# Order of the constants at the start of attention, and the place of the next expert's count

## The chip, the cores and the metric

The kernel runs on one core of a Trainium2 chip. The metric is the device time of one execution in microseconds (us); the median over several runs is compared. A profile of one further execution shows what each engine did: TensorE (PE; its weight loads are shown apart as PEld), VectorE (DVE), ScalarE (ACT), GpSimd (POOL) and the queue of SyncE (SP), which issues most transfers. A name with a q behind it (PEldq, ACTq) is the engine's sequencer, which fetches instructions, branches and loads registers.

## What is computed

Attention with a window and a few sink tokens, and behind it a mixture of experts with one expert for each token:

```python
# q, k, v: (4, 8, 768, 64); n_sink 4, window 128
scores = q @ k.T / 8
keep = (key < n_sink) | ((query - key >= 0) & (query - key < window))
a = softmax(where(keep, scores, -1e9))
x = (a @ v) as (3072, 512)              # token by token, heads side by side

logits = x @ w_gate                     # (3072, 8)
e = argmax(logits); gate = softmax(logits)[e]
y = gate * (relu(x @ w1[e]) @ w2[e])    # w1: 512 x 1024, w2: 1024 x 512
```

All of it is float32. A product in the experts is made of three: each operand is split into a high part (rounded) and the rest, and high x high, high x rest and rest x high are added.

## The kernel before

**Attention.** The 3072 tokens are 24 groups of 128 queries (`g`), and each group has 8 heads in two quads. For a head TensorE computes the scores into one of four PSUM banks `s` (`qk`, L189); VectorE scales them, applies a mask and takes the row's extreme in one custom instruction into `smask` (`softmax`, L203); ScalarE takes the exponential (`exp`, L210); TensorE transposes the result (`tp`, L231) and multiplies by the values (`pv`, L274). The scores of the next quad need the banks that the softmax step of this quad has read. Behind it come norms, the gate's logits and, for batches of groups, the routing: which expert each token goes to and at which place.

The softmax step needs a mask tile: `m0` for the first block of a sequence, `m1` for the second, `m2` for all others. They are built by VectorE (`Constants.mask`, L467) from `win` and `sk` (`window`, L461), which need the numbers `n_sink` and `window` as floats (`numbers`, L447), which a small DMA brings (`num`, L509), the first of SP's queue. VectorE also makes constants that only later steps use: `routing` (L491: `tri`, `iota8`, `four`, `tok`, `slots`) for the routing, and `vbd` (L499), which the sink values need. GpSimd makes the index patterns (`iotas`, `more_iotas`), fills some tiles (`fills`, L487) and sets `rows0` to zero (L1172), the tile into which the experts' rows are later gathered.

**The planner.** The order of all this is not written by hand. Each step is put into a `Plan` with a rank, the steps it waits for, and a cost for each engine that may do it (`t` TensorE, `v` VectorE, `a` ScalarE, `p` GpSimd, `s` SP). `Plan.order` walks in time over a model with these costs: at each point it takes the engine that can start first, and of the steps ready for it the one with the lowest rank. The instructions are then issued in that order, and each engine runs its own in that order. Steps that become ready at another point of the model may change the order on every engine behind them. The experts' constants have rank 14.5, the masks -7.5, 0.5 and 8.5, the softmax step -3 and more with each head, and the zeroing 18.5.

**The experts.** Behind attention and an early part of expert 0 (256 of its tokens), `run` goes through the 8 experts. The number of tokens of an expert, in units of 32, is known only on the chip. It stands in the tile `m`, and each of the five engines has a register for it. `tc.Switch(R[e], ...)` (L1063) branches to the body that was made for this number (0 to 32 units), on each engine by itself. `load_units(e)` (L813) gives one register load to each of the five engines (L816; the profile calls it TENSOR_LOAD). `regs` loads the count of expert 0 ahead of all bodies, and the body of expert `e` loads the count of expert `e + 1` as its first instruction; the last body loads none.

A body with up to 4 units is `narrow`; up to 16 units it is one `chunk`; with more it is two chunks, the first with `first=True`. A chunk first calls `begin` (evacuation of the previous expert's sums by ScalarE and VectorE, L1005 and L1007, and their scatter by GpSimd, four indirect DMAs, L1037). Then it goes over 8 slices of the hidden dimension: `l1` is 12 products of one slice (L889), a relu on ScalarE (L893) and its rest on VectorE (L895); `l2`, four slices behind, is the second product (L905). Between them `own` and `ahead` split the weights of this or the next expert (ScalarE L666, VectorE L674) and start the next load into the raw tile (SP, L661), and `turn_rows` transposes the rows of the next expert (L872) and, on GpSimd, gathers those of the one after. `narrow` does the same with tokens and hidden dimension exchanged (`first(p)`, L963).

## Time and profile before

| | |
|---|---|
| median of 3 runs | 559.08 us (558.99 to 561.92) |
| the profiled execution | 559.36 us, span 557.6 us |
| granted TensorE clock, mean | 0.969 |
| attention and routing | up to about 208 us |
| early part of expert 0 | to about 223.8 us |
| bodies of experts 0 to 7, first product at | 226.75, 255.60, 323.41, 360.36, 407.36, 443.64, 470.78, 528.86 us |
| last TensorE work to the end of the span | about 16 us |

In the rows shown below a time is in us from the start of the span. A row of the order in time has start, duration, engine, line, operation, output <- inputs and, in brackets, how long the engine was idle before and what the profile holds to have ended that. A row by line (L816) has the count, the shortest, middle and longest duration in ns, and the first and last start. A row of a stretch (A:B) has its length, each engine's busy time with the number of instructions, then the granted clock of TensorE (1.00 is full), the busy share of the DMA engines and GB/s.

### The profile page before, as it was taken

Reading aid. Unit: us, or ns where it says so; the run is one execution under the profiler, and the core shown is the slowest. Engines: PE = TensorE matmul, PEld = TensorE weight load, DVE = VectorE, ACT = ScalarE, POOL = GpSimd, SP = SyncE. Lnnn points to the kernel's source line nnn. Section 1 sums busy time; section 2 is a strip of 40 time slices with the busy share of each in tenths; the row PEclk is TensorE's granted clock in tenths of the full one; section 3 lists DMA queues with packets and bytes.
Section 4 is the critical chain, followed back from the end, with each engine's and each line's share of the span. In section 5 each row is a group of like instructions: output and inputs, shape, how many; then the busy total and the mean of one; then the engine's idle time right before and its main releaser. Section 6 shows DMA issues by size and latency. Waiting matters only on the chain.

```text
span 557.6 us, 12015 instructions
## 1 busy us (share of the span) xinstructions
PE 513.3 (92%) x4182; PEld 423.8 (76%) x4182; DVE 325.0 (58%) x1105; ACT 289.3 (52%) x813; POOL 127.5 (23%) x171
## 2 busy tenths in 40 slices
PE   5999999999999899798999989899989898999980
PEld 3667777777777688787989789788788696998670
DVE  8797788888797955463316356264156283526230
ACT  2889888988988812353215254263155172425240
POOL 3222330120104414425012032121032133210020
PEclk9899999999999999799999999999989999999996
DMA  8778764543432106474106436254247375310010
GB/s 261 239 253 250 224 192 143 148 146 117 142 113 59 39 21 204 140 229 118 58 19 205 136 132 203 87 183 127 66 136 256 93 237 151 103 42 2 8 46 21
DMA packets 48494, 74.57 MB, mean 134 GB/s; under 512 B 7130, under 2 KB 19418, under 8 KB 48288
## 3 DMA queue, kind: packets, MB, share of 16 engines
q1 hardware_dynamic: 42208, 59.05, 33.7%
q0 software_dynamic: 6080, 13.39, 8.1%
q14 instruction: 151, 1.24, 0.9%
q8 instruction: 55, 0.90, 0.8%
HBM read 63.23 MB, written 15.73 MB: 142 GB/s over the span
## 4 chain that ended last, share of the span: by engine, by line
PE 69%; issue 10%; DVE 7%; DMA 7%; ACT 5%; POOL 1%; another core or an unknown queue 0%; DVEq 0%; ACTq 0%; POOLq 0%
PE hp L889 23%; PE y L905 20%; DMA out<-ys,oi 7%; PE s L189 6%; PE pt L231 6%; PE xps L274 6%; PE tp L872 2%; ACT pn L210 2%; PE xps L290 2%; PE m L286 1%; ACT ptc L140 1%; DVE wl L674 1%; PE m L410 1%; DVE smask L203 1%; PE xps L261 1%
## 5 line engine op out<-in xcount | busy, mean ns | idle before, releaser
L889 PE MATMUL hp<-xh,wh 128*128 128x288 f32 (+6 forms) x288 | 93.9, 326 | 14.2 <-DVE ys L1005 7.5
L210 ACT ACTIVATE pn<-smask,sm 128x260 f32<-128x260 f32 (+1 forms) x192 | 92.7, 485 | 16.5 <-DVE sm L203 16.1
L674 DVE TENSOR_TENSOR wl<-wraw,wh 128x512 fp32r<-128x512 f32 x117 | 81.0, 706 | 26.1 <-ACT wh L666 23.3
L889 PE MATMUL hp<-xh,wl 128*128 128x288 f32 (+6 forms) x288 | 92.7, 322 | 0.0
L889 PE MATMUL hp<-xl,wh 128*128 128x288 f32 (+6 forms) x288 | 92.6, 322 | 0.0
L905 PE MATMUL y<-wh,hh 128*128 128x512 f32 (+2 forms) x224 | 91.1, 407 | 0.0
L893 ACT ACTIVATE hh<-hp 128x256 fp32r<-128x256 f32 (+6 forms) x80 | 34.2, 428 | 108.1 <-PE hp L889 100.7
L905 PE MATMUL y<-wh,hl 128*128 128x512 f32 (+2 forms) x224 | 88.1, 393 | 0.0
L905 PE MATMUL y<-wl,hh 128*128 128x512 f32 (+2 forms) x224 | 87.9, 392 | 0.0
L895 DVE SCALAR_TENSOR_TENSOR hl<-hp,hh 128x256 fp32r<-128x256 f32 (+6 forms) x80 | 38.1, 477 | 79.8 <-ACT hh L893 70.4
L666 ACT ACTIVATE wh<-wraw 128x512 fp32r<-128x512 f32 x116 | 70.5, 625 | 25.0 <-PE y L905 24.2
L889 PEld LDWEIGHTS hp<-xh,wh 128*128 128x128 f32 x288 | 58.2, 202 | 20.1 <-issue 17.2
L203 DVE CUSTOM_DVE_ANT_0 smask<-s,m 128x260 f32<-128x260 f32 (+1 forms) x192 | 69.3, 398 | 6.6 <-PE s L189 4.8
L1037 POOL DMA_INDIRECT out<-ys,oi x34 | 34.9, 1025 | 155.4 <-ACT ys L1007 147.0
L889 PEld LDWEIGHTS hp<-xl,wh 128*128 128x128 f32 x288 | 58.0, 201 | 2.1
L889 PEld LDWEIGHTS hp<-xh,wl 128*128 128x128 f32 x288 | 57.9, 201 | 0.9
L189 PE MATMUL s<-keys,q 64*64 64x196 f32 (+2 forms) x768 | 52.1, 346 | 5.5 <-DVE sm L203 5.1
L858 POOL DMA_INDIRECT rows<-rows,tl x32 | 32.6, 1018 | 86.5 <-PE tp L872 70.8
L231 PE MATMUL pt<-ident,pn 128*128 128x128 f32 x352 | 49.1, 280 | 0.8 <-ACT pn L210 0.3
L905 PEld LDWEIGHTS y<-wh,hl 128*128 128x128 f32 (+2 forms) x224 | 39.5, 176 | 12.2
L905 PEld LDWEIGHTS y<-wl,hh 128*128 128x128 f32 (+2 forms) x224 | 39.7, 177 | 10.1
L905 PEld LDWEIGHTS y<-wh,hh 128*128 128x128 f32 (+2 forms) x224 | 39.6, 177 | 9.2
(207 smaller groups left out, 758.2 us busy)
## 6 DMA issues: line engine op xcount, KB each, us to landing
wraw<-in_w SPq DMA_DIRECT2D x128, 256.0 KB
keys<-in_k SPq DMA_DIRECT2D x24, 264.0 KB
q<-in_qp SPq DMA_DIRECT2D x24, 256.0 KB
v<-in_v SPq DMA_DIRECT2D x24, 256.0 KB
rows<-row SPq DMA_DIRECT2D x24, 256.0 KB
out<-ys,oi POOLq DMA_INDIRECT x34
rows<-rows,tl POOLq DMA_INDIRECT x32
vs<-in_vs SPq DMA_DIRECT2D x4, 24.0 KB
```

What stands on the lines that cost most here:

```text
L189: nc.tensor.matmul(self.s[h % 4][o, a:z], self.q[g][rows, hp, o], self.keys[rows, hp, at + a:at + z], start=True, stop=True)
L203: nc.vector.tensor_tensor_reduce(t[:, :w], s[:, :w], m, -0.125, 3.0e38, OP.add, OP.min, sm[:, 0, h:h + 1])
L210: self.nc.scalar.activation(self.pn[g][:, h, :w], t[:, :w], AF.Exp, bias=sm[:, 0, h:h + 1], scale=-1.0, accum_out=sm[:, 1, h:h + 1])
L231: nc.tensor.transpose(t[:, h % 2, j, :], self.pn[g][:, h, c:c + 128], self.cons["ident"])
L274: nc.tensor.matmul(self.xps[r * 64:(r + 1) * 64, hp, :], self.v[g + d][:, h * 64:(h + 1) * 64], t[:, r, j, :], start=(j == 0 and hp == 0), ...
L666: self.nc.scalar.activation(w, r, AF.Copy)
L674: {"v": self.nc.vector, "p": self.nc.gpsimd}[e].tensor_tensor(w, r, self.wh[k][:, u % FT].bitcast(F32), op=OP.subtract)
L889: nc.tensor.matmul(p[:, :n], w[:, dd], x[b][:, d, :n], start=(i == 0), stop=(i == 11))
L893: nc.scalar.activation(hh[:, :n], p[:, :n], AF.Relu)
L895: nc.vector.scalar_tensor_tensor(hl[:, :n], p[:, :n], 0.0, hh[:, :n].bitcast(F32), op0=OP.max, op1=OP.subtract)
L905: nc.tensor.matmul(y, h[:, j * 128:j * 128 + w], x, start=(f == 0 and k == 0), stop=(f == FT - 1 and k == 2))
L1037: st = nc.gpsimd.indirect_dma_start(out=self.out, out_offset=bass.IndirectOffsetOnAxis(ap=ids[:, j:j + 1], axis=0), in_=self.ys[k][:, j, : ...
```

## The change

Three steps of the plan get one more step to wait for. The experts' constants `routing` and `vbd` wait for the third mask, `("m", 2)`; the zeroing of `rows0` waits for the first exponential of group 1, `("exp", 1, 0)`. Costs and ranks stay as they are. And `load_units(e + 1)` goes from the head of `expert` into `chunk`, behind `l1` of slice 0 of the first chunk, and into `narrow`, behind `first(0)`.

```diff
-        put(("c", "route"), self.routing, "c", 14, [("c", "rel"), ("c", "more"), ("c", "fill")], args=(), v=500)
-        put(("c", "vbd"), self.vbd, "c", 14, [("c", "more")], args=(), v=1600)
+        put(("c", "route"), self.routing, "c", 14, [("c", "rel"), ("c", "more"), ("c", "fill"), ("m", 2)], args=(), v=500)
+        put(("c", "vbd"), self.vbd, "c", 14, [("c", "more"), ("m", 2)], args=(), v=1600)
...
         for f in range(FT):
             if n:
                 self.l1(e, f, b, n)
+            if first and f == 0:
+                self.load_units(e + 1)
             if first and 1 <= f <= BEHIND:
                 self.own(e, FT - BEHIND - 1 + f)
...
         self.begin(e)
         first(0)
+        self.load_units(e + 1)
         for f in range(FT - BEHIND, FT):
             self.own(e, f)
...
     def expert(self, e, m):
         last = e + 1 == E
-        self.load_units(e + 1)
         nxt = None if last else (0, (e + 1) % 2, 4)
...
-    put(("zero",), lambda: moe.nc.gpsimd.memset(moe.rows[0], 0.0), "w1", 0, args=(), p=2500)
+    put(("zero",), lambda: moe.nc.gpsimd.memset(moe.rows[0], 0.0), "w1", 0, [("exp", 1, 0)], args=(), p=2500)
```

## The prediction

> **What bounds the kernel now.** I read the page first, then the table of stretches, then the instructions in order of time, last the sequencer's own instructions by line. On the page TensorE is busy for 92% of the span, and the chain that ended last is 69% TensorE and 10% "issue".

> ```profile
> span 557.6 us, 12015 instructions
> ...
> PE 513.3 (92%) x4182; PEld 423.8 (76%) x4182; DVE 325.0 (58%) x1105; ACT 289.3 (52%) x813; POOL 127.5 (23%) x171
> ...
> PE 69%; issue 10%; DVE 7%; DMA 7%; ACT 5%; POOL 1%; another core or an unknown queue 0%; DVEq 0%; ACTq 0%; POOLq 0%
> ```

> The stretches show where TensorE is not full: early, and with a clock of 0.69. From 20 us on it is nearly full, so whatever is won ahead of that should be carried to the end.

> ```profile
> 9.00:20.00 11.00, 9.19 (x80) 6.30 (x80) 8.52 (x46) 7.24 (x30) 3.29 (x4) 0.69 0.82 268
> 20.00:60.00 40.00, 38.06 (x499) 28.58 (x499) 33.70 (x165) 35.04 (x125) 12.35 (x17) 1.00 0.82 250
> 60.00:180.00 120.00, 117.67 (x1551) 90.72 (x1547) 100.66 (x486) 102.63 (x360) 22.08 (x47) 1.00 0.48 142
> ```

> In the experts TensorE waits only at the first product of a body (223 to 530 us): 7.5 + 6.7 us at seven bodies, 1.3 us at the eighth. The releaser "DVE ys" is only the last other event before the idle time ended; no row shows TensorE held by it.

> ```profile
> PE hp L889 <- DVE ys L1005: 7.5, 4, 2.1
> PE hp L889 <- issue: 6.7, 3, 2.9
> PE hp L963 <- DVE ys L1005: 1.3, 1, 1.3
> ```

> **Part 1: masks ahead of the experts' constants.** VectorE's queue at the start, with the other engines' rows beside it:

> ```profile
> 0.75 0.39 SPq L509 DMA_DIRECT2D num<-in_nums  x1
> ...
> 1.92 2.21 DVE L501 CAST vf<-vi 32x8 f32<-32x8 int32 x1
> ...
> 2.30 1.80 POOL L1172 MEMSET rows<- 128x2048 f32 x1
> ...
> 4.54 1.28 DVE L505 COPY vbd<-vf 32x512 f32<-32x512 f32 x3
> ...
> 5.56 0.67 PE L189 MATMUL s<-keys,q 64*64 64x128 f32 x16
> 5.85 0.17 DVE L449 CAST numf<-num 128x4 f32<-128x4 int32 x1
> ...
> 6.53 0.22 DVE L493 TENSOR_SCALAR tri<-rel 128x128 bf16<-128x128 f32 x1
> ...
> 6.99 0.35 DVE L463 TENSOR_SCALAR win<-rel,nums 128x256 f32<-128x256 f32 x1
> ...
> 9.05 0.28 DVE L203 CUSTOM_DVE_ANT_0 smask<-s,m 128x128 f32<-128x128 f32 x1
> ...
> 17.12 0.62 POOL L670 TENSOR_SCALAR wh<-wraw 128x512 fp32r<-128x512 f32 x1 [4.78 <-DMA wraw<-in_w]
> ```

> VectorE begins on the window numbers at 5.85, right behind vbd, and on the first softmax step at 9.05, though its scores were done at 5.56 + 0.67 = 6.23. From numbers to softmax it is 9.05 - 5.85 = 3.20, of which routing is 6.99 - 6.53 = 0.46; without it 2.74. When the numbers land isn't shown: between the end of their issue (1.14) and 5.56, since the scores' keys and queries were issued behind them on the same queue. So the first softmax step comes between 6.3 (the scores) and 5.56 + 2.74 = 8.30, a gain of 2.75 to 0.75. Numbers that land by 3.6 give it all, and they are the first transfer of the queue: I take 2.75.

> Against it: routing and vbd are still to be done, 0.46 + 1.66 (from 4.16, where the stretched cast ends, to 5.82) + some 0.3 for the cast = 2.4 on VectorE, now inside the softmax of the first groups. VectorE has 11.00 - 8.52 = 2.48 us idle between 9 and 20 us, in pieces. I take half as hidden and half as exposed, **-2.75 + 1.2 = -1.6**. All exposed and the numbers late it is -0.75 + 2.4 = +1.65; all hidden, and the 1 us of half clock and waits behind it shortened too, -3.75. Those are the bounds.

> The third edit puts the zeroing, 1.80 us on GpSimd, behind the first exponential of group 1. Behind it in that queue stand the routing's copies and the weight splits, the first of which waits 4.78 us for its DMA; that wait hides it, and without it 1.8 us would fall on GpSimd, not on the chain. But the cast of 8 elements took 2.21 us beside this zeroing, so the same can befall a VectorE copy there: 0 to 1.8, priced as a rival. No DMA issue moves. The planner may order later steps otherwise; with 38.06 + 117.67 of 160 us busy TensorE has 4.3 us to win or lose there, and I take 0.

> **Part 2: the loads of the next count.** Each body sends one load to each of five sequencers.

> ```profile
> L816 PEldq TENSOR_LOAD <-m x8: 304/314/495, 215.9 to 470.3; - x8
> ...
> L816 PEldq TENSOR_LOAD <-m x1: 307/307/307, 406.8 to 406.8; - x1
> ...
> 407.32 0.28 PEld L889 LDWEIGHTS hp<-xh,wh 128*128 128x128 f32 x1 [2.49 <-issue]
> ...
> L1063 PEldq BRANCH_PREFETCH_HINT  x1: 36/36/36, 528.7 to 528.7; - x1
> ...
> 528.83 0.19 PEld L963 LDWEIGHTS hp<-wh,xh 128*128 128x128 f32 x1 [1.81 <-issue]
> ...
> 215.80:216.50 0.70, 0.70 (x6) 1.00 1.20 346
> ```

> At 406.8 the load stands between the branch and the first weights at 407.32. The last body has no load (there is no next expert): there the weights come at once behind the branch's hint. So the load costs at least its own 0.31; at most, by the gaps, (14.2 - 2.9)/6 - 1.3 = 0.58 (the first body left out, its 2.9 has another cause too). Between them I take 0.43, times seven bodies: **-3.0** (0 to -4.1).

> Moved behind the first slice, it stands on TensorE behind twelve products. Those are queued when it runs: the load at 215.9 ran while TensorE was busy for 0.70 of 0.70 us. The slice lasts 12 products, over 1.2 us even at 192 columns (of the 1.40 us with x12 below), and covers it; uncovered it costs 0.43 again. On ScalarE and VectorE it passes the evacuation and the first relu and its rest, and there it delays the split behind, at most 0.3 us each:

> ```profile
> 445.41 0.33 ACT L893 ACTIVATE hh<-hp 128x192 fp32r<-128x192 f32 x1 [2.36 <-PE hp L889]
> 445.64 0.62 ACT L666 ACTIVATE wh<-wraw 128x512 fp32r<-128x512 f32 x1
> ```

> The 0.33 of the relu hides nearly all, and the split's result is used an expert later. On GpSimd the load passes four scatter issues, which wait for ys in either place and come 0.3 sooner at most. SP has nothing in between, so its weight loads keep their place.

> **Part 3: what the shorter gap does to the clock.** Stretches of 3.41 us, from the one that holds a gap (the columns are busy time of each engine, then granted clock):

> ```profile
> 253.77:257.18 3.41, 1.58 (x9) 1.61 (x10) 0.00 (x0) 0.60 (x2) 2.35 (x3) 1.00 0.59 136
> 257.18:260.59 3.41, 3.41 (x22) 3.41 (x21) 1.87 (x3) 1.66 (x5) 2.43 (x3) 1.00 0.41 139
> 403.95:407.37 3.42, 1.36 (x7) 0.72 (x5) 1.41 (x2) 1.27 (x2) 0.94 (x1) 1.00 0.00 0
> 407.37:410.78 3.41, 3.41 (x13) 3.41 (x14) 0.00 (x0) 0.00 (x0) 2.48 (x4) 0.50 0.47 177
> 410.78:414.19 3.41, 3.41 (x25) 3.41 (x24) 2.13 (x4) 2.40 (x5) 0.59 (x1) 1.00 0.36 124
> 441.50:444.91 3.41, 1.40 (x12) 1.30 (x12) 1.41 (x2) 1.27 (x2) 1.78 (x2) 1.00 0.21 73
> 444.92:448.32 3.40, 3.40 (x19) 3.40 (x17) 1.05 (x2) 1.19 (x4) 2.22 (x3) 0.50 0.38 133
> 448.32:451.73 3.41, 3.41 (x32) 3.41 (x32) 3.17 (x7) 3.17 (x8) 0.18 (x1) 1.00 0.51 161
> 468.81:472.22 3.41, 1.62 (x13) 1.48 (x13) 0.00 (x0) 0.17 (x1) 2.49 (x3) 1.00 0.57 112
> 472.22:475.63 3.41, 3.41 (x18) 3.41 (x18) 1.78 (x4) 1.82 (x5) 2.23 (x3) 0.50 0.44 156
> 475.63:479.04 3.41, 3.41 (x31) 3.41 (x31) 2.20 (x4) 1.59 (x4) 1.97 (x2) 1.00 0.31 100
> 526.83:530.25 3.42, 2.09 (x16) 1.53 (x14) 1.41 (x2) 1.27 (x2) 0.98 (x1) 1.00 0.05 16
> ...
> 226.46:233.29 6.83, 6.54 (x31) 6.57 (x32) 1.58 (x4) 1.75 (x4) 2.34 (x3) 0.50 0.41 147
> ```

> Experts 4, 5 and 6 start at half clock: a stretch with 1.36, 1.40 or 1.62 us of TensorE work in 3.41 is followed by one at 0.50. With 1.58 (expert 1) and 2.09 (expert 7) the clock stays. So the border lies near 1.6 us of work, or 1.8 us idle. A gap shorter by 0.43 leaves 1.36 + 0.43 = 1.79, 1.83 and 2.05, all above it. Half clock costs, by the products done against the stretch behind: 3.41 x 12/25 = 1.6, 3.41 x 13/32 = 1.4, 3.41 x 13/31 = 1.4, together 4.4. Bounds: all of it stays (0), or the first expert's two stretches go too, 6.54 x 0.5 = 3.3 at most. VectorE has 0.24 us idle in 448.32 to 451.73, so some of expert 5's 1.4 may turn into a wait for it. I take **-4.4**.

> [...]

> **Sum.** -1.6 - 3.0 - 4.4 = -9.0. The profiled execution took 559.36 (span 557.6), 0.28 above the median of 559.08: 550.4 in its terms, **550.1** against the median.

> **Rivals.** *The clock doesn't follow the gap*: half-clock stretches stay as many. For it: 1.58 and 1.62 us of work lie side by side and were followed by 1.00 and 0.50. Against: 1.36 and 1.40 fell low, 2.09 did not. 550.1 + 4.4 = 554.5. *The start gives it back*: vbd and routing stand between scores and softmax of group 1, and the zeroing locks a copy: -2.75 + 2.4 + 1.8 = +1.45 in place of -1.6, 553.1. For it: the 2.21 us cast; against: the 2.48 us idle. *Expert 0 is helped too*: its gap falls from 2.9 to 2.5 and its two stretches go, 3 us: 547.1. Against: 2.5 is still above 1.8. *It doesn't do what it says*: "DVE ys" does hold the first product, gaps and clock stay: 559.1 - 1.6 = 557.5. Against: the last body, whose weights follow its hint at once and whose wait bears the same name. *Slower*: the load drains TensorE in mid-body. Then each of seven bodies pays the 0.43 again and about 0.13 to restart (528.7 to 528.83), +1.0 over now, and the second pause falls into the same 3.41 us as the first: experts 1 to 3 drop to half clock too, 3 x 1.6. With -1.6 at the start that is +4.2, 563.3. It decides as soon as the load starts behind the last queued product. Against: 0.70 of 0.70.

> **Chances.** Forecast 50%, clock stays 22%, start gives back 9%, expert 0 too 9%, no effect of the loads 6%, drain 4%. What can be told from no change is about 0.5%, 2.8 us: below 556.3 is faster, above 561.9 slower. Faster: the first four, less 3 for mixtures, 87%; same 9%; slower 4%. The range holds the first four: from 546.0 (expert 0 and 1 us more at the start) to 556.5 (clock stays and the start gives back in part).

> **What would show it.** The first softmax step by 7 us; the first weights within 0.2 us of the hint at every body; TensorE's idle gaps at 1.3 to 1.7 us (2.5 at the first); no idle of TensorE between first and second slice; no 0.50 behind experts 4 to 6. I am wrong if the start of the experts' phase (223.8 us) doesn't move, if the gaps stay at 2 us, or if 0.50 stands behind gaps of 1.6.

## The result, and the profile after

The changed kernel took **550.71 us** (median of 4, 548.94 to 553.7) beside 559.78 us for the kernel before on the same chip: a ratio of **0.984, interval 0.981 to 0.988**, or about 9 us. Two later comparisons on other chips gave 0.986 (0.980 to 0.993) and 0.982 (0.975 to 0.988). The 14 times of the three have a middle of 550.6 us and reach from 547.4 to 555.5; the kernel before reached from 554.3 to 566.9. That spread belongs to the finding, as the clock shows below. A ratio here is taken over executions within 1.5% of the fastest of their kernel (a longer one counts as slow), so it can differ from the quotient of two medians.

The execution profiled first took 553.7 us, the longest of its four. On its page the span and TensorE's busy time fell together, and a transfer that the page before didn't name stands in the chain that ended last (the last row: lines of the chain with their share of the span):

```profile
span 551.9 us, 12018 instructions
...
PE 508.2 (92%) x4181; PEld 418.6 (76%) x4182; DVE 322.3 (58%) x1104; ACT 290.3 (53%) x815; POOL 127.4 (23%) x170
...
DMA out<-ys,oi 25%; DMA rows<-rows,tl 10%; PE y L905 7%; PE hp L889 7%; PE xps L274 6%; PE s L189 6%; PE pt L231 5%; DMA vs<-in_vs 2%; DVE smask L203 2%; PE xps L290 2%; PE m L286 1%; ACT pn L210 1%; PE m L410 1%; PE xps L261 1%; PE tp L872 1%
```

That transfer is `vs`, the sink values. The 25% and 10% of the scatters and gathers are where the way back leads over GpSimd's queue; no wait of TensorE listed below names them.

**Attention, in order of time** (start, duration, engine, line, operation, in brackets the idle time before and what ended it):

```profile
2.41 0.17 DVE L449 CAST numf<-num 128x4 f32<-128x4 int32 x1 [0.56 <-DMA num<-in_nums]
...
6.01 0.29 DVE L203 CUSTOM_DVE_ANT_0 smask<-s,m 128x128 f32<-128x128 f32 x1 [0.66 <-PE s L189]
...
15.24 1.81 POOL L1174 MEMSET rows<- 128x2048 f32 x1
...
15.38 1.70 DVE L216 TENSOR_SCALAR sm<-sm 128x8 f32<-128x8 f32 x1
...
38.40 0.19 DVE L167 CAST vh<-vs 96x64 fp32r<-96x64 f32 x1 [1.99 <-DMA vs<-in_vs]
...
40.55 0.38 PE L189 MATMUL s<-keys,q 64*64 64x196 f32 x2 [2.88 <-DVE sm L203]
...
227.37 0.34 PE L889 MATMUL hp<-xh,wh 128*128 128x224 f32 x1 [2.75 <-issue]
```

The softmax starts at 6.01 instead of 9.05 and is bound by its scores there. The zeroing does stretch a VectorE operation beside it: 8 elements for each row take 1.70 us (0.17 us in `e9` below, without the zeroing beside them). The operation began 0.14 us behind the zeroing and ended 0.03 us behind it (15.38 + 1.70 = 17.08; 15.24 + 1.81 = 17.05).

Then the lead is lost. Of the 3 us, 2.2 are left at group 4 (softmax at 33.44 after 35.60), and at group 8 the changed kernel is 1.2 us behind (67.75 after 66.57). At 36.4 us VectorE comes to the cast of the second batch's sink values and stands there for 1.99 us, because `vs` hasn't landed; TensorE, which needs the softmax behind it, then idles for 2.88 us, and a stretch at 0.50 follows (42.09, below). Expert 0's first product comes at 227.37, 0.6 us *later* than before (226.75). So in this execution the start gave nothing against the profile before, in which VectorE didn't wait for `vs`.

**The experts.** What TensorE waited for from 200 to 530 us (releaser: sum, times, longest), and the stretches of 3.41 us that hold a gap, with the one behind (busy time of PE, PEld, DVE, ACT, POOL, then the granted clock):

```profile
PE hp L889 <- issue: 5.5, 3, 2.7
PE hp L889 <- ACT ys L1010: 3.6, 3, 1.3
PE hp L889 <- DVE hl L895: 3.0, 1, 3.0
PE hp L889 <- DVE ys L1008: 1.6, 1, 1.6
PE hp L965 <- ACT ys L1010: 1.1, 1, 1.1
PE y L975 <- DVE hl L978: 0.7, 1, 0.7
```

```profile
38.67:42.09 3.42, 1.54 (x17) 0.80 (x17) 3.15 (x13) 2.43 (x8) 2.20 (x2) 1.00 0.53 174
42.09:45.50 3.41, 3.41 (x24) 3.08 (x24) 1.60 (x8) 3.38 (x13) 0.62 (x1) 0.50 0.67 231
...
400.49:403.90 3.41, 2.11 (x11) 1.46 (x10) 1.41 (x2) 1.27 (x2) 0.75 (x1) 1.00 0.00 0
403.90:407.31 3.41, 3.41 (x25) 3.41 (x24) 1.09 (x2) 1.19 (x3) 2.47 (x4) 1.00 0.42 159
434.62:438.03 3.41, 2.28 (x14) 1.55 (x13) 1.41 (x2) 1.26 (x2) 0.82 (x1) 1.00 0.05 12
438.03:441.44 3.41, 3.41 (x32) 3.41 (x32) 1.56 (x4) 2.20 (x5) 2.21 (x3) 1.00 0.40 154
465.34:468.75 3.41, 0.45 (x3) 0.45 (x4) 2.24 (x5) 0.90 (x2) 1.11 (x2) 1.00 0.26 96
468.75:472.17 3.42, 3.42 (x18) 3.42 (x17) 1.10 (x3) 0.90 (x2) 2.17 (x2) 0.50 0.33 99
```

Experts 4 and 5 (400 and 434 us) now have 2.11 and 2.28 us of work in the stretch with the gap, and the one behind does 25 and 32 products at full clock, where it did 13 and 19 before. Expert 6 kept a stretch at 0.50, for a new reason: its gap fell to 1.29 us, but six microseconds later TensorE waited 2.97 us for VectorE's `hl`. In all, 324.5 us pass from expert 0's first product to the end instead of 330.8.

### The profile page after: what moved, and what is told of

Read it like the earlier page. It is cut to its first block, busy times and chain, and to the rows that moved or that the text cites. A ratio compares the mean times of both kernels' runs of the same rounds, so it can differ in the third digit from the quotient of the medians.

```text
span 551.9 us, 12018 instructions
## 1 busy us (share of the span) xinstructions
PE 508.2 (92%) x4181; PEld 418.6 (76%) x4182; DVE 322.3 (58%) x1104; ACT 290.3 (53%) x815; POOL 127.4 (23%) x170
## 4 chain that ended last, share of the span: by engine, by line
PE 38%; DMA 37%; issue 11%; DVE 7%; ACT 2%; POOL 1%; SPq 1%; POOLq 0%; another core or an unknown queue 0%; DVEq 0%; ACTq 0%
DMA out<-ys,oi 25%; DMA rows<-rows,tl 10%; PE y L905 7%; PE hp L889 7%; PE xps L274 6%; PE s L189 6%; PE pt L231 5%; DMA vs<-in_vs 2%; DVE smask L203 2%; PE xps L290 2%; PE m L286 1%; ACT pn L210 1%; PE m L410 1%; PE xps L261 1%; PE tp L872 1%
## 5 line engine op out<-in xcount | busy, mean ns | idle before, releaser
L889 PE MATMUL hp<-xh,wh 128*128 128x288 f32 (+6 forms) x288 | 91.2, 317 | 13.8 <-issue 5.5
L889 PE MATMUL hp<-xh,wl 128*128 128x288 f32 (+6 forms) x288 | 89.8, 312 | 0.0
L889 PE MATMUL hp<-xl,wh 128*128 128x288 f32 (+6 forms) x288 | 89.8, 312 | 0.0
L893 ACT ACTIVATE hh<-hp 128x256 fp32r<-128x256 f32 (+6 forms) x80 | 34.1, 427 | 101.8 <-PE hp L889 98.8
L666 ACT ACTIVATE wh<-wraw 128x512 fp32r<-128x512 f32 x116 | 70.5, 626 | 25.8 <-PE y L905 25.0
L203 DVE CUSTOM_DVE_ANT_0 smask<-s,m 128x260 f32<-128x260 f32 (+1 forms) x192 | 69.0, 398 | 8.3 <-PE s L189 6.0
L889 PEld LDWEIGHTS hp<-xh,wh 128*128 128x128 f32 x288 | 55.2, 192 | 20.1 <-issue 13.8
L889 PEld LDWEIGHTS hp<-xl,wh 128*128 128x128 f32 x288 | 55.3, 192 | 2.1
L889 PEld LDWEIGHTS hp<-xh,wl 128*128 128x128 f32 x288 | 55.2, 192 | 0.9
L189 PE MATMUL s<-keys,q 64*64 64x196 f32 (+2 forms) x768 | 50.5, 339 | 5.9 <-DVE sm L203 5.5
L231 PE MATMUL pt<-ident,pn 128*128 128x128 f32 x352 | 50.4, 283 | 1.1 <-ACT ptc L140 0.3
```

The costliest lines, as they stand in the source:

```text
L189: nc.tensor.matmul(self.s[h % 4][o, a:z], self.q[g][rows, hp, o], self.keys[rows, hp, at + a:at + z], start=True, stop=True)
L203: nc.vector.tensor_tensor_reduce(t[:, :w], s[:, :w], m, -0.125, 3.0e38, OP.add, OP.min, sm[:, 0, h:h + 1])
L231: nc.tensor.transpose(t[:, h % 2, j, :], self.pn[g][:, h, c:c + 128], self.cons["ident"])
L666: self.nc.scalar.activation(w, r, AF.Copy)
L889: nc.tensor.matmul(p[:, :n], w[:, dd], x[b][:, d, :n], start=(i == 0), stop=(i == 11))
L893: nc.scalar.activation(hh[:, :n], p[:, :n], AF.Relu)
```

## The experiments

Each is compared with the kernel before on its own chip. Because executions differ by more than the terms in question, the profile of each run is read too; the table at the end puts them side by side.

**One part alone.** `e1` moves only the loads, `e2` only the steps of the plan:

```diff
# e1, against the kernel before
+            if first and f == 0:
+                self.load_units(e + 1)
...
         first(0)
+        self.load_units(e + 1)
...
     def expert(self, e, m):
-        self.load_units(e + 1)
# e2, against the kernel before
-        put(("c", "route"), ..., [..., ("c", "fill")], ...)
-        put(("c", "vbd"), ..., [("c", "more")], ...)
-    put(("zero",), ..., "w1", 0, args=(), p=2500)
+        put(("c", "route"), ..., [..., ("c", "fill"), ("m", 2)], ...)
+        put(("c", "vbd"), ..., [("c", "more"), ("m", 2)], ...)
+    put(("zero",), ..., "w1", 0, [("exp", 1, 0)], args=(), p=2500)
```

> The kernel before with one part of the change: each expert's body loads the next unit count behind its first slice of products instead of at its head; masks, constants and zeroing are as before. Theory A (the prediction's terms for the experts): -3.0 us of register loads and -4.4 us of half clock, so about 7.4 us below the kernel before, with TensorE's gaps at the heads of experts 1 to 7 at 1.1 to 1.7 us and no clock of 0.50 behind experts 4 and 5; expert 6 keeps one stretch of half clock if, as in the trace after, its first products wait for VectorE's scaling of hl (2 to 3 us), which takes about 1.5 us back: 6 to 7.5 us. Rival B (the clock doesn't follow the gap): -3.0 us. Rival C (the loads were hidden): within 0.5 us of before.

Measured: 555.79 us against 560.76, ratio 0.994 (0.990 to 0.997). Its profile has the gaps of theory A (1.2 to 1.6 us at experts 1 to 6) and no stretch at 0.50 behind any of these; from expert 0 to the end it takes 323.7 us, 7.1 less than before. But its attention, which wasn't touched, lost 2 us on the way:

```profile
39.70 0.19 DVE L167 CAST vh<-vs 96x64 fp32r<-96x64 f32 x1 [1.07 <-DMA vs<-in_vs]
...
41.90 0.38 PE L189 MATMUL s<-keys,q 64*64 64x196 f32 x2 [2.00 <-DVE sm L203]
```

So the wait for `vs` isn't made by the earlier softmax; it is a close race there in either order. By the profile theory A holds for the experts. By the times, which have that race in them, its 6 to 7.5 us don't fit in the interval (1.5 to 5.4 us), and rival B's 3.0 do; what speaks against B is the profile: between 220 and 530 us it has one stretch at 0.50, behind expert 0, where the kernel before had five.

> The kernel before with the other part alone: routing and vbd wait for the third mask and the zeroing for the exponential of group 1; the unit counts are loaded at each body's head as before. Theory A (from the trace after): the softmax starts 3.0 us earlier, the lead is 2 us still at group 4, and is lost between 36 and 42 us, where VectorE stands with the cast of vs for a transfer issued at 34 us (2 us of waiting) and a stretch of half clock follows; the experts' phase starts within 1 us of before, and the whole is within 1 us of before. Rival B (the prediction): 1.6 us faster. Rival C: the loss in the trace after came from that execution alone: no wait for vs above 0.5 us, and 1.5 to 3 us faster.

Measured: 558.38 us, ratio 0.990 (0.983 to 0.996), six times that lie at 551.9 to 553.6 and at 557.6 to 560.5. The profiled one is of the upper group, and in it the wait and the gap are there:

```profile
37.92 0.19 DVE L167 CAST vh<-vs 96x64 fp32r<-96x64 f32 x1 [2.16 <-DMA vs<-in_vs]
...
40.10 0.59 PE L189 MATMUL s<-keys,q 64*64 64x196 f32 x2 [3.08 <-DVE sm L203]
```

Theory A's picture is right for that execution, and its total is wrong: over the executions the start is worth more than 1 us, and the interval (2.2 to 9.4 us) leaves the prediction's 1.6 out too. That rests on few times, two of them far below the others; `e12` below is the firmer run.

**The price of a load.** A first try repeated the load at each head (`self.load_units(e + 1)` twice):

> The kernel before with the unit count of the next expert loaded twice at each body's head, one load after the other: the disputed cost doubled. Theory A (a load on TensorE's path costs 0.42 us at each head, and the clock follows the gap): gaps of experts 1 to 7 at 1.7 to 2.5 us, +2.5 to +3.0 us for the loads, and one or two more stretches of half clock (1.5 us each): +3 to +6 us. Rival B (the clock doesn't follow): +2.5 to +3 us with the same stretches at 0.50 as before. Rival C (hidden loads): no change.

It measured 560.65 us, ratio 1.000 (0.996 to 1.004), and it tells nothing of the price: both loads wrote the same register, and the program that ran held one (the row has eight loads on TensorE, as before). It is one more look at the kernel before.

```profile
L816 PEldq TENSOR_LOAD <-m x8: 300/308/492, 215.5 to 468.7; - x8
```

The second try loads two counts into two registers at experts 0, 2 and 4, the last one at expert 6, and none at odd experts:

```diff
         last = e + 1 == E
-        self.load_units(e + 1)
+        if e % 2 == 0:
+            self.load_units(e + 1)
+            self.load_units(e + 2)
```

> The kernel before with the same eight loads paired: the bodies of experts 0, 2, 4 and 6 load two unit counts at their head, one behind the other (into different registers), those of 1, 3, 5 and 7 none. Theory A (a load at the head costs 0.42 us of TensorE's gap, and the clock is halved for the next 3.41 us where TensorE is idle for over 1.8 us within one window of that length, as in the six traces so far): gaps at experts 2, 4 and 6 of 2.0 to 2.5 us, at 1, 3, 5 and 7 of 1.1 to 1.7 us; stretches at 0.50 behind those of 2, 4 and 6 whose gap lies within one window, none behind 1, 3, 5 and 7; the whole within 2 us of before. Rival B (the load is no part of the gap, as the doubled load would have it if it had stood twice): all gaps at 1.6 to 2.1 us as before. Rival C (the gap isn't what halves the clock): stretches behind odd experts too.

Measured: 562.35 us against 562.09, ratio 1.001 (0.996 to 1.005). The heads of experts 2 (two loads) and 3 (none), from the branch's last instruction (the hint) to the first product:

```profile
L1065 PEldq BRANCH_PREFETCH_HINT  x1: 40/40/40, 328.4 to 328.4; - x1
...
L816 PEldq TENSOR_LOAD <-m x2: 305/306/308, 328.5 to 329.0; - x2
...
329.46 0.42 PE L889 MATMUL hp<-xh,wh 128*128 128x384 f32 x1 [1.86 <-DVE ys L1005]
...
L1065 PEldq BRANCH_PREFETCH_HINT  x1: 40/40/40, 365.9 to 365.9; - x1
...
366.06 0.45 PE L889 MATMUL hp<-xh,wh 128*128 128x480 f32 x1 [1.33 <-ACT ys L1007]
```

Two loads cost 329.46 - 328.4, or 1.0 us (the trace has 328.45 for the hint), none 0.2 us (365.85): 0.4 us for each. The heads of all 14 profiles agree: 0.20 to 0.26 us from hint to first product without a load, 0.60 to 0.71 with one, 1.00 to 1.05 with two. Rival B is gone as to this stretch behind the branch. The gaps themselves came only in part as theory A has them: 1.33, 1.12 and 1.57 at experts 3, 5 and 7 and 2.05 at expert 4, but 1.86 at expert 2, below its 2.0 to 2.5 (expert 6, with one load, had 1.90). And expert 1 had 2.40 us without a load, because TensorE's branch took 5.76 us there where the other seven took 4.4 to 4.9. Behind it stood 0.50, so rival C is not what this shows: the gap was long, only the load wasn't the reason.

**The changed kernel again**, for a second and a third profile:

> The changed kernel once more, for a second profile. If what the first profile showed belongs to the kernel: VectorE waits about 2 us for vs near 36 to 40 us with a stretch of half clock behind it, and TensorE waits 2 to 3 us for hl of expert 6 with another; 550.7 us as before. If it belongs to that one execution (the longest of its four): neither, and a profiled time near 549 us.

> The changed kernel, as a neighbour for e6 on this chip and for a third profile. Theory A: the times fall in two groups, near 549 us where VectorE's wait for vs stays under 1 us and near 553 us where it is over and the clock is halved behind it; the profile says which of the two its own execution is. Rival: one group.

`e4`: 552.84 us, profiled at 548.99. VectorE waited 0.37 us for `vs`, TensorE idled for 0.98 us and no 0.50 followed. The lead was kept to the end of attention, expert 0 at 223.54, 3.2 us before the kernel before:

```profile
36.00 0.19 DVE L167 CAST vh<-vs 96x64 fp32r<-96x64 f32 x1 [0.37 <-DMA vs<-in_vs]
...
37.87 0.38 PE L189 MATMUL s<-keys,q 64*64 64x196 f32 x2 [0.98 <-DVE sm L203]
...
223.54 0.34 PE L889 MATMUL hp<-xh,wh 128*128 128x224 f32 x1 [2.46 <-issue]
```

`e8`: 550.38 us, profiled at 550.14, and with the wait again:

```profile
38.13 0.19 DVE L167 CAST vh<-vs 96x64 fp32r<-96x64 f32 x1 [2.63 <-DMA vs<-in_vs]
...
40.31 0.38 PE L189 MATMUL s<-keys,q 64*64 64x196 f32 x2 [3.55 <-DVE sm L203]
```

Of the two losses in the first profile, the wait for `vs` thus belongs to the kernel, though not to each execution; VectorE's `hl` at expert 6 came back with 0.3 us at most in these two. Its 2.97 us are a matter of that execution, but shorter waits for `hl` behind a body's first products, of 0.2 to 1.0 us, stand in most profiles with the load moved, and in `e2`. The two groups of times that `e8`'s theory wanted aren't there (547.4, 548.5, 550.1, 550.6, 550.6, 554.6): the wait doesn't make a group by itself, for this profile with the wait lies in the middle of them: it had no stretch at 0.50 from 45 to 530 us.

**The wait for `vs` taken away.** `e6` (on the changed kernel), `e7` (on the kernel before) and `e12` (on `e2`) load the sink values of the next batch three groups earlier, into buffers of their own:

```diff
-            if i == 0:
-                vs = self.pw.tile([96, D], F32, name="vs", bufs=1)
-                nc.sync.dma_start(vs, io["vs"][b])
-                self.vsr = vs
+            if g == 0 or i == 3 and b + 1 < B:
+                n = b + 1 if g else 0
+                vs = self.p1.tile([96, D], F32, name=f"vs{n}")
+                nc.sync.dma_start(vs, io["vs"][n])
+                self.vsr[n] = vs
```

> The changed kernel with the sink values of the next batch loaded three groups earlier, into buffers of their own (the DMA is issued with v of group 3, 9 and 15). Theory A (the lead of 3 us is lost to VectorE's wait for vs and the half clock behind it): no wait for vs beyond the start, no TensorE gap above 1 us near 40 us and no 0.50 there, the lead of 2.5 to 3 us is there still at group 8 (softmax at 64 us) and at the experts' start (223.5 to 224 us), and the times lie near 549 us with the executions at 552 to 555 us gone: 548 to 550 median. Rival B (another transfer is as late as vs: keys, q or the weights): the gap near 40 us is there as before with another name, and 550.5 to 553 us.

> The kernel of e6 once more, as the neighbour of e9 and e10 on this chip: the softmax at group 8 at 64.2 us, experts' start at 223.5 to 224 us, no wait for vs behind the start; 550 to 551.5 us. If its median is 548.5 to 549.5, the clock behind expert 0 (two windows at 0.50 in e6's profile) is what kept e6 from showing the 3 us.

The mechanism of theory A held: no wait, no gap above 1 us near 40 us, and expert 0 at 223.83 (224.59 in `e11`, whose profile is of its longest time).

```profile
35.85 0.17 DVE L169 CAST vh<-vs 96x64 fp32r<-96x64 f32 x1
...
223.83 0.52 PE L891 MATMUL hp<-xh,wh 128*128 128x224 f32 x1 [2.68 <-issue]
```

The total did not: 551.17 us (ratio 0.985) and 552.74 us (0.985), where the changed kernel beside `e6` took 550.38 (0.982). Both profiles of this kernel had two stretches at 0.50 behind expert 0, the three of the changed kernel none; the 3 us gained ahead of the experts can be lost to the clock behind them (two stretches are 2.9 us at the 1.44 us each that the 14 profiles show below). The expected medians (548 to 550 us, and for `e11` 550 to 551.5) were missed. That the earlier load makes the kernel faster isn't shown.

> The kernel before with the same earlier load of the sink values and nothing else. Theory A: the wait for vs was there in some executions of the kernel before too (e1, whose attention is the same, had 1.1 us of it and a stretch of half clock), so that these vanish: 557.5 to 559 us against 560.8, and the difference to e6 is the change's own effect without that wait: 9 to 10 us. Rival B (the wait belongs to the earlier softmax alone): within 0.7 us of before.

> The kernel of e2 (masks first, unit counts loaded at each body's head) with the earlier load of the sink values of e6: the start alone without the wait for vs. Theory A (the start is worth 2.9 us where nothing is late behind it, the loads and the clock the rest): no wait for vs behind 30 us, first product of expert 0 at 223.9 to 224.6 us against 226.8 to 227.5 in the profiles with the masks behind and no wait; from there to the end 329 to 332 us as in the four profiles with one load at the heads, with three to five stretches at 0.50; ratio to before 0.99 to 0.994. Rival B (e2's ratio of 0.990 came from elsewhere: the start is worth nothing once the wait is gone): expert 0 at 226.5 us or later.

`e7`: 558.57 us against 562.09, ratio 0.997 (0.993 to 1.001). The interval holds 1, so neither of its theories is shown, and `e6` is 7.4 us below it instead of 9 to 10. `e12`: 555.13 us against 561.00, ratio 0.993 (0.989 to 0.996), expert 0 at 223.59, and 329.1 us from there on with four stretches at 0.50, as theory A has it (expert 0 another 0.3 us earlier than its range):

```profile
223.59 0.34 PE L891 MATMUL hp<-xh,wh 128*128 128x224 f32 x1 [3.04 <-issue]
```

The start by itself is worth about 3 us where nothing is late behind it: with a wait for `vs` of 0.4 us at most, expert 0 begins at 226.75, 226.92 and 227.48 with the masks behind, and at 223.54, 223.83, 224.59 and 223.59 with the masks first (the first three of these without a load at expert 0's head, which is 0.4 of it). The clock has a share in it: between 8 and 19 us the five profiles with the masks behind have two or three stretches at 0.50, the nine with the masks first one or none. How much of the 3 us that is, these runs don't separate.

**Two more parts, of the gap and of the zeroing.** `e9` lets the zeroing of `e6` wait in the plan for the third mask, `("m", 2)`, instead of `("exp", 1, 0)`. `e10` adds to `e9` eight products of the zero tile, ahead of the experts:

```diff
+        for y in self.y[EARLY // 128:] * 4:
+            nc.tensor.matmul(y, self.warm_t[:, :128], self.warm_t, start=True, stop=True)
         self.hh += self.more[0]
```

> The kernel of e6 with the zeroing of the rows released by the third mask instead of group 1's exponential, so that GpSimd writes it near 8 us, when VectorE waits, and not at 15.3 us over VectorE's normalization of group 0. Theory A (VectorE's L216 of 1.70 us for 8 elements is held by the zeroing, and VectorE is on the path there): L216's counterpart takes 0.2 us, the softmax of groups 2 to 8 starts 1 to 1.6 us earlier than in e6, and the time falls by as much: 549 to 550 us. Rival B (the 1.5 us have slack behind them, or the lock moves to the constants): the softmax at group 8 within 0.4 us of e6, no change.

`e9`: 549.76 us (ratio 0.982, 0.977 to 0.988) beside 552.74 for `e11`, six times each that overlap. The zeroing didn't go where the expectation put it. A step of the plan sets an order, not a wait, and GpSimd had nothing to wait for: it ran at 2.31, and the cast of the numbers took 1.66 us beside it (0.17 in the profiles before and after).

```profile
2.31 1.80 POOL L1176 MEMSET rows<- 128x2048 f32 x1
...
2.47 1.66 DVE L451 CAST numf<-num 128x4 f32<-128x4 int32 x1 [0.63 <-DMA num<-in_nums]
...
15.29 0.17 DVE L218 TENSOR_SCALAR sm<-sm 128x8 f32<-128x8 f32 x1
```

Whether that is the cheaper place isn't settled. The softmax starts at 6.8, where the profiles with the later zeroing have 6.0 to 7.1. At group 8 it stands at 62.8 in `e9` and at 63.8 in `e10`, whose attention is the same; `e12`, `e4`, `e6` and `e11`, with the zeroing near 15 us and little or no wait for `vs`, have 63.6, 64.2, 64.2 and 64.8. On the mean that is 0.9 us for the later zeroing, but the two groups overlap, and the totals show no difference.

> The kernel of e9 with eight products of the zero tile (128x512) more, queued on TensorE ahead of expert 0's switch into banks that aren't in use there. Theory A (the gap at expert 0, 2.7 us, is the branch of 4.2 to 4.8 us less the work queued on TensorE when its sequencer gets to the branch, and a gap under 1.8 us keeps the clock): gap at expert 0 of 1.3 to 1.8 us, no 0.50 behind it in any window, first product of expert 0 0.5 to 1 us later than in e9; 0 to 2.5 us faster than e9 by whether e9's own executions have the stretches behind expert 0. Rival B (the sequencer gets to the branch as much later as the fill lasts): the gap stays at 2.5 to 2.9 us, 1.8 us slower.

`e10`: 550.06 us (ratio 0.981), no different from `e9`. The gap at expert 0 fell with the fill, from 3.03 in `e9` to 0.99 us, below the 1.3 to 1.8 that theory A expected, and no 0.50 stands behind it. Expert 0 comes 0.8 us later than in `e9` (222.68), and at group 8 this execution was 1.0 us later already; rival B's gap of 2.5 to 2.9 us isn't there:

```profile
220.56 1.90 PE L1058 MATMUL y<-warm 128*128 128x512 bf16 x8
...
223.45 0.34 PE L891 MATMUL hp<-xh,wh 128*128 128x224 f32 x1 [0.99 <-issue]
```

In the profiled execution experts 5 and 6 fell to 0.50 instead (gaps of 1.63 and 2.78 us), the second one because its branch took 6.13 us:

```profile
L1243 PEldq COMPARE_BRANCH  x16: 320/2235/6132, 219.0 to 533.2; - x16
```

**All profiles** (us; worked out from their traces: wait for `vs` at 35 to 41 us, start of expert 0's first product, from there to the end of the span, stretches of 3.41 us at 0.50 between 220 and 530 us):

| | wait for vs | expert 0 | rest | at 0.50 |
|---|---|---|---|---|
| masks behind, load at the head: before, e3 | 0, 0.3 | 226.75, 226.92 | 330.8, 329.5 | 5, 4 |
| the same, vs early: e7 | 0 | 227.48 | 331.8 | 5 |
| masks behind, pairs of loads: e5 | 2.0 | 232.16 | 327.2 | 3 |
| masks behind, load moved: e1 | 1.1 | 228.87 | 323.7 | 1 |
| masks first, load at the head: e2 | 2.2 | 228.25 | 329.1 | 4 |
| the same, vs early: e12 | 0 | 223.59 | 329.1 | 4 |
| the change: first profile, e4, e8 | 2.0, 0.4, 2.6 | 227.37, 223.54, 226.64 | 324.5, 323.7, 321.7 | 1, 1, 0 |
| the change, vs early: e6, e11 | 0, 0 | 223.83, 224.59 | 325.1, 328.8 | 2, 4 |
| the same and the zeroing early: e9 | 0 | 222.68 | 324.4 | 1 |
| the same and the fill: e10 | 0 | 223.45 | 326.4 | 2 |

## Why the prediction was right, point by point

**The total**, 550.1 us against a measured 550.7, was right, and it was nearer than its terms were; that nearness is luck, as the spread of the 14 times (547.4 to 555.5) says already.

**The loads** were right. Predicted at 0.43 us a head; `e5` measures 0.4, with two, one and no load at a head. Behind the first slice the load is hidden: after the change no wait of TensorE stands between a body's first and second slice, and the first product comes 0.20 to 0.26 us behind the hint at every body. Gaps of 1.3 to 1.7 us were predicted; at experts 1 to 6 they are 1.1 to 1.6 us in the first profile, and up to 2.1 in the two later ones.

**The clock** was right in kind and in the price of a stretch; which stretches go was luck. The border of about 1.8 us idle in 3.41 held (of the stretches with 1.78 to 1.90 us idle 9 of 15 were followed by 0.50, and from 1.93 us on 26 of 26), and the stretches behind experts 4 and 5 are gone. The price can be read from TensorE's busy time between expert 0's first product and expert 7's, which holds the same products in every kernel. Three of the 14 profiles, the kernel before with 4.9 stretches at 0.50 in that time, `e4` with one, `e8` with none (the second number is the length, the third TensorE's busy time):

```profile
226.75:528.86 302.11, 289.55 (x1601) 250.56 (x1601) 137.07 (x230) 117.64 (x231) 61.96 (x62) 0.97 0.39 124
...
223.54:518.35 294.81, 284.16 (x1601) 244.52 (x1601) 136.93 (x230) 117.65 (x231) 62.70 (x62) 0.99 0.41 127
...
226.64:519.94 293.30, 282.32 (x1600) 242.98 (x1601) 137.09 (x230) 117.97 (x231) 62.72 (x62) 1.00 0.41 127
```

A straight line through all 14 rises by **1.44 us a stretch**, and none lies more than 0.42 us off it: the prediction's 1.4 to 1.6. The number of stretches differs from one execution to the next. The five profiles with one load at each head have 4.4 of them and take 330.1 us from expert 0's first product to the end; the seven with the load moved and no fill have 1.4 and take 324.6. Of these 5.5 us, 4.1 are busy time, which is the clock. The gaps at the heads of experts 1 to 7 fell from 12.5 to 10.2 us, which is 2.3 for six loads, and TensorE's waits for VectorE's `hl` grew from 0.2 to 1.2 us, which takes 0.9 back. So the clock's term is 4.1, or **3.2 with these waits, instead of 4.4**. The waits are what the remark that expert 5's 1.4 us may turn into a wait for VectorE named; whether the load's new place in VectorE's queue adds to them, no run here separates. And the three stretches that went aren't the predicted three: 0.7 of them stood behind expert 0, which the forecast left out, and the other four profiles with the load at the heads have none to two behind experts 4 to 6. These means are of 12 profiles that scatter by several microseconds.

**The start** was wrong in size, and in the first profile in effect. Half of the 2.4 us of constants was to be exposed; with no wait for `vs` nothing of that shows, since the first softmax step leads by 2.0 to 2.8 us there (`e4`, `e6`, `e11`, `e12`) and expert 0 by about 2.9. The step that failed is "from 20 us on [TensorE] is nearly full, so whatever is won ahead of that should be carried to the end". TensorE, busy for 38.06 of 40.00 us from 20 us on in the profile before, didn't carry the lead by itself; what feeds it must be in time too. In the eight profiles with the old place of `vs`, VectorE is at its cast 2.4 to 3.0 us behind the transfer's issue with the masks behind (38.56 after 35.60 in the profile before) and 2.2 to 2.6 us with the masks first (36.4 after 33.99). The transfer lands 3.0 to 4.9 us behind its issue, and at most 3.0 in the profile before. So the earlier softmax took only some 0.4 us off the margin, and how long the transfer takes decides the rest. Why it takes 3.0 us in one execution and 4.9 in another isn't shown; the DMA engines were 0.79 to 0.86 busy from 20 to 40 us in all eight. The prediction looked at VectorE's idle time and the zeroing for what might give the lead back, and never at the transfers behind. Its rival named the operation stretched by the zeroing rightly (1.70 us), but priced it in the wrong place of the sum: in `e4` it takes 1.70 us as well, and 3.2 us arrive at expert 0 all the same. So the start is worth **3 us without the wait**, and an execution with the wait gains about nothing on one of the kernel before without it. The kernel before has the wait too: with it, expert 0 began at 228.87 (`e1`) and 232.16 (`e5`), and with the masks first at 226.64 to 228.25. The wait was above 1 us in three of the four profiles with the masks first and the old place of `vs`, and in two of the four with the masks behind. How often it comes in the executions that weren't profiled stays open, and with it the start's mean share; by the times of `e2` it is more than the 1.6 us predicted, by the first profile less.

**By the prediction's own list of what would show it**: the softmax by 7 us, yes (6.0 to 7.1 in the three profiles of the change); no 0.50 behind experts 4 to 6, two of three in the first profile and in `e4`, all three in `e8`; "wrong if the start of the experts' phase doesn't move": in the first profile it moved the wrong way, and in `e4` by 3.2 us; 0.50 behind a gap of 1.6, in no profile of the change and once in `e10` (1.63). The whole came out because the errors of the terms lie on both sides: the clock with its new waits brought less than its 4.4, and the start, by the race, anything from nothing to 3.2 around its 1.6. As shares of the time, `e1` (-0.6%) and `e2` (-1.0%) add up to the whole (-1.6%), with a split other than predicted, which these intervals can't fix.

## What to carry to other kernels

In this kernel a lead won at the start arrived only where the transfers behind it were in time as well: follow the next in-order wait for a DMA on each engine, here a 96x64 tile (VectorE waited 0.4 to 2.6 us for it in the three profiles of the change), and look at its margin in more than one profile, before a gain is carried to the end of the sum. Where a gap lay near the border at which the clock fell here (1.78 to 1.90 us idle in a stretch of 3.41), a few tenths of a microsecond were worth more than their own length on average (4.1 us of clock beside 2.3 us of gaps), but each single execution drew anew (0 to 5 stretches at 0.50 in the 14 profiles), so the number of stretches is read from several profiles; the price of one is read from the engine's busy time. A plan's dependency moves an instruction in its queue, it doesn't hold it back; look where it will really run (the zeroing of `e9` at 2.31 us) and what it stretches there (a cast from 0.17 to 1.66 us).

## What the runs showed of the hardware

**The price of a stretch.** For a stretch of 3.41 us at 0.50 TensorE needed 1.44 us more for the same work, by the 14 profiles above.

**The switch's branch.** TensorE's branch into a body took 3.9 to 6.1 us in these profiles, in one execution of the changed kernel (`e4`) 3.9 to 5.5. The spread is larger than the load that the change removes. With more work queued on TensorE ahead of the branch the gap was shorter: in `e10`, 1.90 us more of it left 0.99 us of expert 0's gap, where `e9` had 3.03.

**The zeroing beside VectorE.** Beside a zeroing of 1.81 us on GpSimd (first profile) a VectorE operation of 8 elements for each row took 1.70 us, and beside one of 1.80 us (`e9`) one of 4 elements took 1.66 us, each 0.17 us without it; they ended 0.03 and 0.02 us behind the zeroing.
